# First weight slab in one load, one small row through the GpSimd queue, and a column transpose two matmuls later

## The chip, the cores and the metric

The kernel runs on one core of one Trainium2 chip. The metric is device microseconds (us) of one execution. Executions of one kernel mostly agree within 0.3%, which here is 0.6 us (the kernel before lay between 213.50 and 214.17 us in the first four runs, and between 213.33 and 213.96, 213.54 and 213.99, 213.58 and 214.00 in three later sets), and the whole change is worth less than that; so this case is also about how to measure and explain something as small as the noise.

## The reference, cut to what matters

```python
x = A_x                                        # (1, 2048, 640)
g = sigmoid((x * gate_w).sum(-1, keepdims=True))
a = ssm(x, ...)                                # a diagonal state-space scan, projections with B and C
b = gelu(x @ w1 + b1) @ w2 + b2                # w1 (640, 1728), w2 (1728, 640)
return g * a + (1 - g) * b
```

Only the first use of `x @ w1`, for the first 512 of 2048 rows of x, matters here.

## The kernel before

The program lists operations with their inputs, outputs and priorities; a small scheduler in the kernel's own code turns them into one fixed order for each engine. Work starts with loads. SyncE issues the big ones in this order: two of five column blocks of x, slab 0 of W1 in two halves, slabs 1 and 2, the other three blocks of x by a transposing load, then slabs 3 and 4. ScalarE issues five small rows. A slab is 128 rows of W1, 1024 columns wide (256 KB).

```python
load("xna", "sp", "l_xna", xn[0][:, :, 0:KN * 128], ..., ["xna"], 0, ...)
for h in range(2):
    fs = slice(h * FW // 2, (h + 1) * FW // 2)
    load(f"w1_0{h}", "sp", f"l_w10{h}", W1sb[:, 0, fs], B_w1[0:128, fs], [("w1", 0, h)], 0.1 + h, ...)
w1load(1, "sp", 1.3)
w1load(2, "sp", 2)
xtrans(0, range(KN, KD), 3, 1.8)
w1load(3, "sp", 4)
w1load(4, "sp", 5)
# ... cut ...
for i, (nm, (r0, src)) in enumerate(ROWS.items()):      # lre, lim, ldt: 5 x 128; b1a: 13 x 128
    src = src.rearrange("(k p) -> k p", p=128)
    load(nm, "act", "l_" + nm, rows[r0:r0 + src.shape[0], :], src, [nm], prio=-100 + i, dur=0.4)
load("b1b", "act", ..., ["b1b"], prio=-96, dur=0.4)      # the last 64 values of b1, twice, into one row
```

TensorE first runs seven warm-up matmuls on a constant, then transposes the two loaded blocks of x (VectorE copies them to `xT`), then begins the 40 matmuls of the first W1 stage. One further transpose, the "column transpose" (`cols`), turns the gathered rows into the per-partition columns that the activations and tables need. It waits for all five row loads.

```python
def f_warm():
    for n in (512,) * 6 + (256,):
        t = nc.tensor.matmul(PS[4][:, 0:n], one.broadcast_to([128, 128]), one.broadcast_to([128, n]), ...)
# ... cut ...
op("cols", "pe", 0.3, list(ROWS) + ["b1b", "ident"], [("bank", 7)], f_cols, prio=9.5)
# ... cut: the first W1 stage, slab by slab (k), eight column blocks (jf) in eight PSUM banks ...
seq = [(k, jf) for k in range(KD) for jf in range(NW)]
seq.remove((0, NW - 1))
seq.insert(seq.index((1, NW - 1)), (0, NW - 1))         # bank 7 is used by the column transpose first
for k, jf in seq:
    op(f"m1_0_{jf}_{k}", "pe", d_mm(512), XK0[k] + [("w1", k) if k else ("w1", 0, jf // (NW // 2))], [("bank", jf)],
       f_mm, prio=pe_prio())
```

So the order on TensorE is: 7 matmuls with slab 0, 2 with slab 1, the column transpose, 7 more with slabs 0 and 1, and then, as the **17th matmul**, the first that needs slab 2 and the transposed rest of x.

## Time and profile before

| | before |
|---|---|
| median of the first 3 runs | 214.07 us (213.73 to 214.17) |
| span of the profiled run (it was timed at 214.2 us) | 212.9 us |
| TensorE (PE) busy | 208.4 us, 98% |
| VectorE (DVE), ScalarE (ACT) busy | 188.9 us, 111.3 us |

Three lines of the page of the kernel before: its span, the busy time by engine, and the chain of work that ended last, by engine.

```profile
span 212.9 us, 3113 instructions
PE 208.4 (98%) x1254; PEld 119.8 (56%) x1264; DVE 188.9 (89%) x262; ACT 111.3 (52%) x201; POOL 2.5 (1%) x10
PE 95%; DMA 2%; issue 1%; ACTq 1%; POOL 0%; DVE 0%; POOLq 0%
```

The kernel is bound by TensorE, and the chain goes through a load for 2% of the span only. Where that load stands is told by the same chain in order of time. This is the chain of the kernel before from 2.22 to 10 us (its 16 earlier lines, GpSimd's and ScalarE's first instructions, are cut); columns are start in us, length in us, and what.

```profile
2.22 0.35 ACTq L326
2.56 0.03 issue
2.60 5.08 DMA rows<-in_B_b_dram
7.68 0.14 issue
7.82 0.22 PE ps L432
8.03 2.16 PE ps L621 x10
```

It is the load of the row `b1b`, ScalarE's fifth: issued from 2.60, landed at 7.68. After it come only matmuls, up to VectorE's last output at 210.79. Next, TensorE's timeline of the kernel before up to 10.5 us: start, length, engine, line, operation, shapes and count, and in brackets the idle time before it with what ended it. L401 are the warm-up matmuls, L413 the transposes of x, L621 the first W1 stage, L432 the column transpose.

```profile
0.78 2.93 PE L401 MATMUL ps<-const-bfloat16-1.0 128*128 128x512 bf16 x7 [0.78 <-PEq L962]
3.74 0.65 PE L413 MATMUL ps<-ident,xn 128*128 128x128 bf16 x8
4.64 1.04 PE L621 MATMUL ps<-xT,W1sb 128*128 128x512 bf16 x4 [0.25 <-DVE xT L419]
5.85 0.82 PE L621 MATMUL ps<-xT,W1sb 128*128 128x512 bf16 x3 [0.17 <-DMA W1sb<-in_B_w_dram]
6.92 0.61 PE L621 MATMUL ps<-xT,W1sb 128*128 128x512 bf16 x2 [0.25 <-DMA W1sb<-in_B_w_dram]
7.82 0.22 PE L432 MATMUL ps<-ident,rows 128*128 128x128 bf16 x1 [0.29 <-DMA rows<-in_B_b_dram]
7.87 2.97 PE L621 MATMUL ps<-xT,W1sb 128*128 128x512 bf16 x13
```

TensorE stops four times: for VectorE's copy, for the second half of slab 0 (landed at 5.80), for slab 1 (6.87) and for `b1b` (7.68). The idle times in brackets look small because a matmul's recorded length (0.379 us) overlaps the next one; matmuls that follow each other without a stop start 0.216 us apart, so the nine before the column transpose need 1.94 us and took 3.18. From 7.87 on there is no stop.

### The profile page before, as it was taken

What the parts mean: (1) busy time and instruction counts of PE and PEld (TensorE: products, weight loads), DVE (VectorE), ACT (ScalarE), POOL (GpSimd) and SP (SyncE); (2) the same over time, 40 slices, a digit from 0 to 9 for tenths busy, and PEclk for the clock granted to TensorE, in tenths of its full rate; (3) what the DMA queues carried; (4) which work ended last, traced back from release to release, by engine and by line L of the source; (5) the groups of instructions that cost most, each with busy time, mean ns of one, the idle gap of its engine ahead of it and who ended that gap; (6) DMA issues with size and microseconds to landing.
All of it is one profiled execution on the core that took longest, in us unless ns stands there. A gap on an engine that the chain in (4) does not pass through costs nothing.

```text
span 212.9 us, 3113 instructions
## 1 busy us (share of the span) xinstructions
PE 208.4 (98%) x1254; PEld 119.8 (56%) x1264; DVE 188.9 (89%) x262; ACT 111.3 (52%) x201; POOL 2.5 (1%) x10
## 2 busy tenths in 40 slices
PE   8899999999999999999999999999999999999996
PEld 3344444444467776444466777544446777767773
DVE  2399999999999999999999959999999998999343
ACT  2389556678915324556963233555793444723330
POOL 1000000000000010000000001000000000000000
DMA  5999999998100004100000004000000000000011
GB/s 134 298 284 200 170 208 318 265 222 183 22 0 3 31 31 126 62 0 0 0 3 0 0 34 155 31 31 3 0 0 2 3 31 31 31 3 31 31 34 62
DMA packets 31434, 16.35 MB, mean 77 GB/s; under 512 B 22972, under 2 KB 30652, under 8 KB 31420
## 3 DMA queue, kind: packets, MB, share of 16 engines
q1 hardware_dynamic: 31072, 14.83, 29.2%
q0 software_dynamic: 288, 1.31, 1.9%
q8 instruction: 10, 0.16, 0.3%
q14 instruction: 4, 0.03, 0.0%
q10 hardware_dynamic: 60, 0.01, 0.0%
HBM read 7.63 MB, written 2.62 MB: 48 GB/s over the span
## 4 chain that ended last, share of the span: by engine, by line
PE 95%; DMA 2%; issue 1%; ACTq 1%; POOL 0%; DVE 0%; POOLq 0%
PE ps L771 27%; PE ps L641 22%; PE ps L819 20%; PE ps L684 20%; PE ps L621 3%; DMA rows<-in_B_b_dram 2%; PE ps L785 1%; PE ps L662 1%; ACTq L326 1%; DVE osb L852 0%; POOL io_i L382 0%; PE ps L432 0%; POOL rows L372 0%; POOL st_i L384 0%; POOL st_i L383 0%
## 5 line engine op out<-in xcount | busy, mean ns | idle before, releaser
L771 PE MATMUL ps<-W2sb,Gl 128*128 128x320 bf16 x416 | 59.2, 299 | 0.0
L771 PEld LDWEIGHTS ps<-W2sb,Gl 128*128 128x128 bf16 x416 | 40.3, 98 | 17.1 <-issue 1.1
L641 PE MATMUL ps<-xT,W1sb 128*128 128x512 bf16 x215 | 47.5, 379 | 0.3
L819 PE MATMUL ps<-CT,H 128*128 128x320 bf16 (+2 forms) x320 | 45.4, 299 | 0.0
L724 DVE TENSOR_TENSOR_SCAN W<-atab,V 128x1280 bf16<-128x1280 f32 x16 | 44.3, 2811 | 0.3
L684 PE MATMUL ps<-xT,BT 128*128 128x512 bf16 x196 | 43.1, 379 | 0.3 <-issue 0.2
L819 PEld LDWEIGHTS ps<-CT,H 128*128 128x128 bf16 x320 | 31.3, 98 | 12.2
L799 ACT ACTIVATE E<-ps,g1col 128x320 bf16<-128x320 f32 x32 | 16.3, 526 | 39.7 <-PE ps L771 26.0
L641 PEld LDWEIGHTS ps<-xT,W1sb 128*128 128x128 bf16 x220 | 21.5, 98 | 26.0
L648 ACT ACTIVATE Gl<-ps,cols 128x512 bf16<-128x512 f32 x44 | 29.6, 688 | 10.0 <-PE ps L641 10.0
L684 PEld LDWEIGHTS ps<-xT,BT 128*128 128x128 bf16 x200 | 19.5, 98 | 23.5 <-ACT Gt L670 0.4
L693 ACT ACTIVATE U<-ps 128x512 bf16<-128x512 f32 x40 | 23.8, 597 | 15.0 <-PE ps L684 14.9
L830 ACT ACTIVATE E<-ps,gcol 128x320 bf16<-128x320 f32 x30 | 15.8, 527 | 22.6 <-PE ps L819 22.6
L482 DVE TENSOR_TENSOR osb<-xg,E 128x640 bf16<-128x640 bf16 x15 | 7.3, 487 | 9.2 <-ACT E L830 8.2
L758 ACT ACTIVATE ps<-b2b 128x320 f32<-128x320 bf16 x32 | 14.1, 442 | 1.1
L838 DVE SCALAR_TENSOR_TENSOR xg<-xn,gcol,dsk 128x640 bf16<-128x640 bf16 x16 | 13.9, 883 | 0.4
L598 DVE SCALAR_TENSOR_TENSOR scr<-xn,gwb 128x640 bf16<-128x640 bf16 x16 | 13.2, 823 | 0.4
L482 DVE TENSOR_TENSOR V<-V,W 128x1280 bf16<-128x1280 bf16 x16 | 12.5, 822 | 0.3
L482 DVE TENSOR_TENSOR H<-H,V 128x1280 bf16<-128x1280 bf16 x16 | 12.5, 822 | 0.3
L482 DVE TENSOR_TENSOR V<-mr,U 128x2560 bf16<-128x2560 bf16 x8 | 11.9, 1489 | 0.2
L482 DVE TENSOR_TENSOR H<-c,W 128x2560 bf16<-128x2560 bf16 x8 | 11.9, 1489 | 0.1
L482 DVE TENSOR_TENSOR V<-s,W 128x2560 bf16<-128x2560 bf16 x8 | 11.9, 1485 | 0.0
(79 smaller groups left out, 98.5 us busy)
## 6 DMA issues: line engine op xcount, KB each, us to landing
out_dram<-osb SPq DMA_DIRECT2D x15, 160.0 KB, 1.8
W2sb<-in_B_w_dram SPq DMA_DIRECT2D x1, 2080.0 KB, 9.4
xn<-in_A_x_dram POOLq DMA_DIRECT2D x2, 640.0 KB, 4.7
W1sb<-in_B_w_dram SPq DMA_DIRECT2D x4, 256.0 KB, 4.8
xn<-in_A_x_dram SPq DMA_DIRECT2D x1, 640.0 KB, 8.0
W1sb<-in_B_w_dram SPq DMA_DIRECT2D x1, 480.0 KB, 5.7
W1sb<-in_B_w_dram SPq DMA_DIRECT2D x1, 400.0 KB, 5.8
xn<-in_A_x_dram SPq DMA_DIRECT2D x1, 384.0 KB, 6.2
```

The source lines that it names most:

```text
L482: return inc("dve", nc.vector.tensor_tensor(out=o, in0=a, in1=b, op=o_))
L641: t = nc.tensor.matmul(PS[bank][:, :], W1sb[:, k, jf * 128:(jf + 1) * 128], xT[q][:, k, :], start=(k == 0), stop=(k == KD - 1))
L648: return inc("act", nc.scalar.activation(Gl[q % 2][:, jf, :], PS[bank][:, :], ACT.Gelu_apprx_tanh, bias=b1col[:, jf:jf + 1]))
L684: t = nc.tensor.matmul(PS[bank][:, :], BT[:, ci, kd, k * 128:(k + 1) * 128], xT[q][:, kd, :], start=(kd == 0), stop=(kd == KD - 1))
L693: return inc("act", nc.scalar.activation(dst, src, ACT.Copy, scale=1.0 if ci == 0 else -1.0))
L724: t = inc("dve", nc.vector.tensor_tensor_scan(out=g[:, ci, :], data0=a, data1=v[:, ci, :], initial=0.0, op0=ALU.mult, op1=ALU.add))
L758: return inc("act", nc.scalar.activation(PS[bank][:, 0:HALF], b2b[:, cols], ACT.Copy))
L771: t = nc.tensor.matmul(PS[bank][:, 0:HALF], Gl[q % 2][:, jf, t4 * 128:(t4 + 1) * 128], W2sb[:, jf, cols], start=False, stop=False, skip_gr ...
L799: return inc("act", nc.scalar.activation(E1[c % NE][:, cols], PS[bank][:, 0:HALF], ACT.Copy, scale=g1col[:, c:c + 1]))
L819: t = nc.tensor.matmul(PS[bank][:, 0:n], H[b % NHB][:, ci, k, s * 128:(s + 1) * 128], CT[:, ci, k, cols], start=(i == 0), stop=(i == 2 * K ...
L830: return inc("act", nc.scalar.activation(E2[c % NE][:, cols], PS[bank][:, 0:HALF], ACT.Copy, scale=gcol[:, c:c + 1]))
L838: return inc("dve", nc.vector.scalar_tensor_tensor(out=xg[c % 2][:, :], in0=xn[q % 2][:, c % 4, :], scalar=gcol[:, c:c + 1], in1=dsk[:, :] ...
```

## The change

The intent: fewer issues on SyncE, so that everything behind slab 0 is issued about 0.5 us earlier; `b1b` no longer last in ScalarE's queue; and the column transpose, which waits for the rows, later in TensorE's order.

```diff
-        for h in range(2):
-            fs = slice(h * FW // 2, (h + 1) * FW // 2)
-            load(f"w1_0{h}", "sp", f"l_w10{h}", W1sb[:, 0, fs], B_w1[0:128, fs], [("w1", 0, h)], 0.1 + h, dur=0.45, lat=2.0)
+        w1load(0, "sp", 1)
 ...
-        load("b1b", "act", "l_b1b", ..., ["b1b"], prio=-96, dur=0.4)
+        load("b1b", "pool", "l_b1b", ..., ["b1b"], prio=-50, dur=1.0)
 ...
-        op("cols", "pe", 0.3, list(ROWS) + ["b1b", "ident"], [("bank", 7)], f_cols, prio=9.5)
+        op("cols", "pe", 0.3, list(ROWS) + ["b1b", "ident"], [("bank", 7)], f_cols, prio=11.5)
 ...
-                op(f"m1_0_{jf}_{k}", "pe", d_mm(512), XK0[k] + [("w1", k) if k else ("w1", 0, jf // (NW // 2))], ...
+                op(f"m1_0_{jf}_{k}", "pe", d_mm(512), XK0[k] + [("w1", k)], ...
```

(Another line, in which later stages name slab 0 as an input, changes in the same way.) The order of instructions also changes in two places far from the start: VectorE's last scan comes after one combination of outputs instead of before it, and ScalarE does one small gate activation one eviction later.

More of the change, by code (lines that the diff above doesn't have):

```diff
@@ L377, in bass_gated_mix__ssm_conv_s5__dense_activation_gelu__prompt_kernel @@
             load(nm, "act", "l_" + nm, rows[r0:r0 + src.shape[0], :], src, [nm], prio=-100 + i, dur=0.4)
-        load("b1b", "act", "l_b1b", rows[RT:RT + 1, :].rearrange("o (a p) -> o a p", a=2),
-             B_b1[nmain:F].rearrange("(o p) -> o p", o=1).unsqueeze(1).broadcast_to([1, 2, FL]), ["b1b"], prio=-96, dur=0.4)
+        load("b1b", "pool", "l_b1b", rows[RT:RT + 1, :].rearrange("o (a p) -> o a p", a=2),
+             B_b1[nmain:F].rearrange("(o p) -> o p", o=1).unsqueeze(1).broadcast_to([1, 2, FL]), ["b1b"], prio=-50, dur=1.0)
         def f_iota():
@@ L622, in f_mm @@
                                                       start=(k == 0), stop=(k == KD - 1)))
-                op(f"m1_0_{jf}_{k}", "pe", d_mm(512), XK0[k] + [("w1", k) if k else ("w1", 0, jf // (NW // 2))], [("bank", jf)] ,
+                op(f"m1_0_{jf}_{k}", "pe", d_mm(512), XK0[k] + [("w1", k)], [("bank", jf)] ,
                    f_mm, prio=pe_prio())
@@ L643, in f_mm @@
                     return inc("pe", t)
-                op(f"m1_{q}_{jf}", "pe", KD * d_mm(512), XT[q] + ([("w1", 0, 0), ("w1", 0, 1)] + [("w1", k) for k in range(1, KD)] if jf < NW else [("w1", "r", int(jf * 128 >= FM))]), [("bank", bank)], f_mm, prio=pe_prio())
+                op(f"m1_{q}_{jf}", "pe", KD * d_mm(512), XT[q] + ([("w1", k) for k in range(KD)] if jf < NW else [("w1", "r", int(jf * 128 >= FM))]), [("bank", bank)], f_mm, prio=pe_prio())
                 def f_ge(jf=jf, bank=bank):
```

## The prediction

> **What bounds the kernel now.** TensorE. The page gives it 208.4 of 212.9 us busy, and the chain of waits is 95% TensorE: from 8.03 us to 210.77 us it is one unbroken run of matmuls with gaps of at most 0.16 us. The change removes no matmul, so only the first 8 us count. In the timeline, W1 matmuls start at 4.64 (released by VectorE's copy), then stop until 5.85 (second half of slab 0), until 6.92 (slab 1) and until 7.82 (the column transpose, which waits for the row b1b: the chain shows 5.08 us of DMA, from 2.60 to 7.68). Nine matmuls at 0.216 us spacing need 1.94 us and took 3.18, so 1.24 us is lost between 4.64 and 7.82.
>
> **What changes.**
> - One issue of about 0.5 us leaves SyncE's queue (each W1 issue took 0.42 to 0.49 us), so slabs 1, 2 and the x transpose are issued about 0.5 us earlier. [...] slab 1, issued at 2.26, landed at 6.87, bound by traffic more than by issue.
> - The first four matmuls lose their early release: half a landed at 4.02, the whole slab will land later. Half b landed at 5.80; I estimate the whole at 5.3 (4.8 to 5.8).
> - b1b leaves ScalarE's queue (0.68 us of issue; its table load, 3.31 to 4.59, starts that much earlier, and has slack) and goes to GpSimd after its index patterns, at about 1.4 us. GpSimd's two x loads took 0.75 to 0.89 us to issue and 1.5 us to their first packet; so first packets near 3, landing near 5 (4 to 6.5) in this traffic. [...]
> - The column transpose comes after 11 matmuls, not 9.
>
> **How much is critical.** The 17th matmul (slab 2) also needs the transposed rest of x, landed at 9.04; it began at 9.38. So gain beyond 0.34 us needs that transpose earlier, too. With slab 0 at 5.3: 16 matmuls (3.46) and the column transpose (0.05) lead to 8.85; the transpose of x, issued 0.5 earlier but in the same traffic, at 8.6 to 9.1. I expect the 17th matmul near 9.0 instead of 9.38: 0.35 us gained. The order of the last scan on VectorE also moves by about 2 us, but its H is ready 8 us before it is used: no effect.
>
> **Predicted: 213.7 us**, range 213.2 to 214.3. Faster by over 2%: 0.01; within 2%: 0.98; slower: 0.01.
>
> **What would show it.** Right: first W1 matmul about 5.3 (later than 4.64), few and shorter stops after it, no wait of the column transpose for b1b, chain of waits starting in a W1 or x load instead of b1b, everything after the 17th matmul shifted by one constant. Wrong: b1b still the last to land; slab 0 landing at or after 5.8; x transpose still at 9.0 with TensorE idle before it.
>
> **What would make it wrong.** The GpSimd load may be slow at its first use (later than 7.6 costs time one for one); the single slab may land no earlier than half b, eating the gain; the earlier table load may collide with the loads.

Slab 0 at 5.3, 16 matmuls (3.46 us) and the column transpose (0.05) come to 8.81 (8.85 stands there); with the transposed x at 8.6 to 9.1 that makes a 17th matmul near 9.0 instead of 9.38, and 0.35 us off the 214.07 us of before is 213.7. The 8.6 to 9.1 "in the same traffic" is the author's estimate; the figure of the trace that stands behind it is slab 1's in `before`: of its 4.61 us from issue to landing, issuing took 0.49.

## The result, and the profile after

| | before | after |
|---|---|---|
| median (4 runs each, taken together) | 213.9 us (213.5 to 214.17) | 213.63 us (213.47 to 213.86) |
| ratio, 95% interval | | 0.999 (0.997 to 1.001) |
| span of the profiled run | 212.9 us | 212.3 us |
| slab 0 landed (before: two halves) | 4.02 and 5.80 us | 4.33 us |
| slab 1, slab 2 landed | 6.87, 7.56 us | 6.40, 7.11 us |
| `b1b` landed | 7.68 us | 4.68 us |
| transposed x landed | 9.05 us | 8.58 us |
| 17th matmul started | 9.38 us | 8.74 us |

A ratio is the mean time of one kernel's fast runs over that of the other's of the same rounds, so it is not quite the ratio of the medians quoted. Times here are rounded; the recorded texts cut some of them (9.047 us stands there as 9.04, 8.186 us as 8.18).

The page of the changed kernel, the same three lines:

```profile
span 212.3 us, 3122 instructions
PE 209.3 (99%) x1264; PEld 120.6 (57%) x1264; DVE 189.2 (89%) x262; ACT 111.3 (52%) x201; POOL 3.0 (1%) x11
PE 99%; DVE 0%; issue 0%
```

(This trace holds 1264 PE records and that of before 1254, with 1264 weight loads in both: ten matmul records of before are missing, so the busy times are not compared.) The chain of the changed kernel in order of time, first 10 us:

```profile
0.78 2.93 PE ps L399 x7
3.71 0.03 issue
3.75 1.03 PE ps L411 x8
4.78 2.99 PE ps L619 x11
7.77 0.06 PE ps L430
7.83 2.37 PE ps L619 x11
```

And TensorE's timeline of the changed kernel, first 10.5 us (L399 is the warm-up, L411 the transposes of x, L619 the W1 stage, L430 the column transpose):

```profile
0.78 2.93 PE L399 MATMUL ps<-const-bfloat16-1.0 128*128 128x512 bf16 x7 [0.78 <-PEq L960]
3.75 1.03 PE L411 MATMUL ps<-ident,xn 128*128 128x128 bf16 x8
4.74 3.03 PE L619 MATMUL ps<-xT,W1sb 128*128 128x512 bf16 x11
7.61 0.22 PE L430 MATMUL ps<-ident,rows 128*128 128x128 bf16 x1
7.67 3.18 PE L619 MATMUL ps<-xT,W1sb 128*128 128x512 bf16 x14
```

All waits for loads are gone: the chain is TensorE alone from 0.78 us, and neither `b1b` nor a slab is in it. The transposing load of x was issued 0.49 us earlier, as SyncE's lines of the two kernels show, the kernel before first:

```profile
3.27 1.54 SPq L333 DMA_TRANSPOSE xT<-in_A_x_dram  x1
2.78 1.49 SPq L333 DMA_TRANSPOSE xT<-in_A_x_dram  x1
```

TensorE's lines hide a second thing. The eight transposes of x took 1.03 us where they took 0.65 before, and eleven matmuls took 3.03 us from 4.74, where eleven at 0.216 us spacing plus the overlap of the last (0.379 minus 0.216) would take 2.54. The starts of single instructions show why: the transposes started 107 ns apart (56 before), and the first W1 matmuls at 4.74, 5.14, 5.57, 5.88 and then every 0.216 us. TensorE ran at half speed until about 5.8 us in this run, and until about 3.8 us in the run of before, with the same warm-up from 0.78 us. The granted clock that the profile lists is 1.00 for both kernels and in every stretch of the first 10 us, but it says nothing here: the traces of these two runs hold no clock record at all, and the profile lists 1.00 all the same, also from 4 to 6 us in the changed kernel, where matmuls started 0.40 and 0.43 us apart. Nine of the 14 traces do hold clock records (not `before`, `after`, `after_again`, `slab_only` and `after_cold`); the first one lies between 3.97 and 9.38 us, in each of the nine where the spacing of the matmuls changes (in `before_again`, for instance, at 5.13). So the spacing is a true reading of the speed.

### The profile page after: what moved, and what is told of

Read it like the earlier page. It is cut to its first block, busy times and chain, and to the rows that moved or that the text cites. A ratio compares the mean times of both kernels' runs of the same rounds, so it can differ in the third digit from the quotient of the medians.

```text
span 212.3 us, 3122 instructions
## 1 busy us (share of the span) xinstructions
PE 209.3 (99%) x1264; PEld 120.6 (57%) x1264; DVE 189.2 (89%) x262; ACT 111.3 (52%) x201; POOL 3.0 (1%) x11
## 3 DMA queue, kind: packets, MB, share of 16 engines
HBM read 7.63 MB, written 2.62 MB: 48 GB/s over the span
## 4 chain that ended last, share of the span: by engine, by line
PE 99%; DVE 0%; issue 0%
PE ps L769 27%; PE ps L639 22%; PE ps L817 20%; PE ps L682 20%; PE ps L619 4%; PE ps L399 1%; PE ps L783 1%; PE ps L660 1%; PE ps L411 0%; DVE osb L850 0%; PE ps L430 0%
## 5 line engine op out<-in xcount | busy, mean ns | idle before, releaser
L639 PE MATMUL ps<-xT,W1sb 128*128 128x512 bf16 x220 | 48.1, 379 | 0.0
L682 PE MATMUL ps<-xT,BT 128*128 128x512 bf16 x200 | 43.8, 379 | 0.0
```

The lines of the kernel that those rows point to most:

```text
L639: t = nc.tensor.matmul(PS[bank][:, :], W1sb[:, k, jf * 128:(jf + 1) * 128], xT[q][:, k, :], start=(k == 0), stop=(k == KD - 1))
L682: t = nc.tensor.matmul(PS[bank][:, :], BT[:, ci, kd, k * 128:(k + 1) * 128], xT[q][:, kd, :], start=(kd == 0), stop=(kd == KD - 1))
```

## The experiments

Three theories were set against each other.

- **A (gates).** The 17th matmul starts when the last of its gates opens: TensorE's own earlier matmuls, slab 1 or 2, the row loads through the column transpose, or the transposed x. The whole time is that start plus a constant.
- **B (clock).** The moment when TensorE reaches full speed differs from run to run and eats the gain.
- **C (noise).** The 0.6 us between the two profiled spans is chance.

Later ones (D, E, F, P, S) are stated with their runs. A ratio's partner is the 9 to 11 runs of the kernel before. Kernels are compared only within the same rounds.

### 1. The changed kernel again: `after_again`

No edit. Expected:

> The changed kernel unaltered, for a firmer ratio and a second look at its start. Its profile had the transposes of x and the first three W1 matmuls at half speed (107 and about 420 ns apart instead of 56 and 216), until about 5.8 us; in the kernel before the full speed came at about 3.8 us. Theory A (gates): the 17th matmul waits for the transposed rest of x (landed 8.58) and the speed matters little; gain 0.5 to 0.7 us every time. Theory B [...] where it is late the 17th matmul starts at 9.0 or later and the gain is gone; then the runs of this kernel spread by 0.5 us or more. Rival C (noise): ratio within 0.999 to 1.001 and no lasting difference of the 17th matmul's start.

Measured: median 213.48 us (213.16 to 213.81), ratio 0.9986 (0.9973 to 0.9998). TensorE's timeline of this run, the first eleven W1 matmuls:

```profile
4.60 1.68 PE L619 MATMUL ps<-xT,W1sb 128*128 128x512 bf16 x7 [0.25 <-DVE xT L417]
6.54 1.04 PE L619 MATMUL ps<-xT,W1sb 128*128 128x512 bf16 x4 [0.26 <-DMA W1sb<-in_B_w_dram]
```

Here TensorE was at full speed from the first transposes (55 ns apart), ran out of work and waited for slab 1 (landed at 6.49), and the 17th matmul started at 8.70, 0.05 us after the transposed x landed (8.65). In the first run of this kernel it was slow until 5.8, waited for nothing, and started the 17th at 8.74, 0.16 us after the transposed x (8.58). So a full speed that comes 2 us later cost at most about 0.1 us: it used up time that would have been spent waiting. B's moment does differ from run to run, but it does not eat the gain. The interval just leaves out 1, so C is weakened but the effect is small.

The wait for the transposed x has no bracket in the timeline and is missing from the chain of waits, which runs on from slab 1's load: a matmul's recorded length of 0.379 us covers any stop of up to 0.16 us. It shows in the start of the 17th matmul, 0.367 us after the 16th, and in the waits of TensorE's weight loads (who waited, for what, us in total, times, longest):

```profile
PEld ps L619 <- DMA xT<-in_A_x_dram: 0.5, 1, 0.5
```

### 2. Each part alone: `slab_only`, `b1b_only`, `cols_only`

`slab_only` takes the first and last hunk of the diff, `b1b_only` the second, `cols_only` the third, each on the kernel before. Expected, in this order:

> Slab 0 in one load, the rest as before. Theory A: slab 0 lands near 4.3 to 4.5, the transposed x about 0.5 us earlier (near 8.6), but the column transpose still stands after 9 matmuls and waits for b1b, which still lands at 7 to 7.7; the 17th matmul starts 1.7 us after that, at 8.8 to 9.4; gain 0 to 0.4 us, most likely 0.1. If b1b lands well before 7 here, its wait was caused by the split slab. C: no change at all.

> b1b through GpSimd, the rest as before. Theory A: b1b lands near 4.7, the column transpose no longer waits; the two halves of slab 0 still land at 4.0 and 5.8, slab 1 at 6.9, so TensorE still stops twice; the 17th matmul is then held by the transposed x at 9.0: gain 0.2 to 0.35 us. C: no change.

> Only the column transpose two matmuls later. Theory A: TensorE does two more matmuls (0.43 us) in the time in which it waited for b1b (landing 7.7), so the column transpose starts at 7.8 as before and five matmuls are left instead of seven; the 17th matmul is then held by the transposed x at 9.0 to 9.1: gain 0.3 us, as much as either other part alone. C: no change.

Measured, with landings from the one profiled run of each:

| kernel | median us | ratio (95% interval) | b1b landed | column transpose | transposed x landed | 17th matmul |
|---|---|---|---|---|---|---|
| `slab_only` | 213.64 | 0.9996 (0.9984 to 1.0009) | 6.78 | 7.08 | 8.19 | 8.65 |
| `b1b_only` | 213.93 | 1.0000 (0.9987 to 1.0014) | 4.28 | 7.38 | 9.08 | 9.13 |
| `cols_only` | 213.61 | 0.9993 (0.9981 to 1.0006) | 7.59 | 7.73 | 8.95 | 9.00 |

`b1b` landed at 6.78 in `slab_only`, earlier than the expected 7 to 7.7. In the profiled runs the gates are where A put them: with `b1b` early, or with two more matmuls ahead of the column transpose, the 17th matmul starts 0.05 us after the transposed x; with the slab alone, it starts after the column transpose and seven matmuls (7.08 + 0.06 + 7 x 0.216 = 8.65). But the slab alone did not meet the gate that A had named for it. The column transpose did not wait for `b1b`: it started 0.216 us after the matmul before it, and its line has no bracket:

```profile
7.08 0.22 PE L430 MATMUL ps<-ident,rows 128*128 128x128 bf16 x1
```

The last gate there was TensorE itself, which ran without a stop but at half speed until about 5.7 us. The timed gains of the parts are not resolved: all three intervals hold 1 and also hold a gain of 0.25 us. The 0.2 to 0.35 expected of `b1b_only` and the 0.3 expected of `cols_only` were not seen in the means.

### 3. Two parts at a time: `slab_cols`, `slab_b1b`

`slab_cols` is the whole change without the `b1b` hunk, `slab_b1b` the whole change without the column hunk. Expected:

> The change without its GpSimd part: slab 0 in one load, column transpose after 11 matmuls, b1b on ScalarE's queue. With slab 0 in one load b1b landed at 6.78 even on ScalarE's queue (7.68 with the split slab), before eleven matmuls are done (7.0 to 7.6). Theory A (the 17th matmul starts when the last of its gates opens, the time is that start plus 203.5 us): the 17th matmul starts at 8.2 to 8.7, as early as in the whole change or up to 0.4 us earlier; time equal to the whole change or 0.1 to 0.4 us less. Rival D (the GpSimd part is needed for the gain): b1b lands at 7.6 again, 17th matmul at 9.0, no better than the column shift alone.

> The change without its column shift: slab 0 in one load and b1b through GpSimd, column transpose after 9 matmuls. Theory A: the rows that stay on ScalarE's queue land at 5.8 to 6.0, nine matmuls are done at 6.6 to 7.1, so nothing waits and the 17th matmul starts with the transposed x at 8.6 to 8.7, as in the whole change: the shift is worth nothing once b1b comes early. Also: slab 1, slab 2 and the transposed x landed 0.4 to 0.5 us later in both looks at the whole change (8.58, 8.65) than in the single-slab kernel (8.18); if the GpSimd load causes that, 8.6 again here; if it was chance, something near 8.2 is as likely.

Measured: `slab_cols` median 213.36 us, ratio 0.9986 (0.9974 to 0.9997); `slab_b1b` 213.33 us, 0.9984 (0.9972 to 0.9996). In their profiled runs the 17th matmul started at 8.64 (transposed x 8.60) and 8.42 (transposed x 8.36; a tie, for TensorE's own matmuls allowed no start before 8.42 either). D falls: with the slab in one load, either of the other two parts gives what both give, as far as these intervals tell, and the GpSimd route is not needed. That the slab alone gives less is not shown: its interval overlaps theirs. The question whether the GpSimd load itself delays the big loads stays open: 8.36 is between the two values that were named.

### 4. The kernel before again: `before_again`

No edit. Expected:

> The kernel before, unaltered, as one of the four: it tells how far two equal kernels differ here, and gives a second look at its start. Its nine runs in the last call spanned 212.0 to 212.6 us, the 17th matmul at 9.38 in the one look belongs to a run of 212.9. Theory A: time minus the 17th matmul's start is 203.5 us here too, so a faster run must show b1b or the transposed x landing earlier (b1b 7.0, 17th matmul 8.7 to 9.0). Ratio within 0.999 to 1.001.

Measured: median 213.75 us, ratio 1.0001 (0.9989 to 1.0013): two equal kernels. One line of TensorE's timeline in this run, the column transpose:

```profile
7.32 0.22 PE L432 MATMUL ps<-ident,rows 128*128 128x128 bf16 x1 [0.29 <-DMA rows<-in_B_b_dram]
```

The wait for `b1b` is there again, with the same 0.29 us in brackets, but everything is 0.5 us earlier than in the first profile: `b1b` at 7.18 (7.68), transposed x at 8.55 (9.05), 17th matmul at 8.88 (9.38), span 212.4 (212.9). This unaltered kernel thus differs from itself by 0.5 us at the start. In both runs the 17th matmul started about 0.33 us after the transposed x, held by `b1b`.

### 5. Another order of the loads: `after_xt_first`

```diff
-        xtrans(0, range(KN, KD), 3, 1.8)
+        xtrans(0, range(KN, KD), 1.9, 1.8)      # on the changed kernel: before slab 2, not after it
```

> The changed kernel with the transposed load of x issued before slab 2 instead of after it. Theory A: the transposed x lands about 0.7 us earlier (near 7.9) and slab 2 then lands last, near 8.4 to 8.7, so the gate moves to slab 2 and the 17th matmul starts at 8.4 to 8.8: no or little gain. If the loads land by issue order at one common rate, the later of the two lands at the same 8.6. A 17th matmul at 8.2 or earlier would say that the transposed load itself, not the sum of the traffic, was the limit.

Measured: median 213.95 us, ratio 1.0006 (0.9993 to 1.0019), with one run at 214.74. The transposed x landed at 7.76, as expected, but slab 2 at 9.80 in the profiled run, so the 17th matmul came at 9.93. TensorE's timeline there:

```profile
7.56 1.24 PE L619 MATMUL ps<-xT,W1sb 128*128 128x512 bf16 x5
9.93 1.24 PE L619 MATMUL ps<-xT,W1sb 128*128 128x512 bf16 x5 [1.13 <-DMA W1sb<-in_B_w_dram]
```

The expected 8.4 to 8.8 was missed by 1.1 us: the loads do not simply share one rate. The transposed load kept SyncE's queue busy from 2.26 to 4.42 us (such a first transposing load took from 1.49 us (`after`) to 2.88 us (`b1b_first`) to issue in ten runs, slabs 0 to 2 and their halves 0.42 to 0.49 us each in `before` and `after`), so slab 2 was issued at 4.47 instead of 2.27, and it landed 5.3 us after that (4.8 us after its issue in the changed kernel). By their spans the other four runs were better (212.3 to 212.9). This is no improvement.

### 6. What stops the W1 loads: `rows_pool`

In the changed kernel all rows go through GpSimd, so ScalarE issues no load early:

```diff
-            load(nm, "act", "l_" + nm, ..., [nm], prio=-100 + i, dur=0.4)
+            load(nm, "pool", "l_" + nm, ..., [nm], prio=-49 + i, dur=0.1)
```

> The changed kernel with all five row loads on GpSimd's queue, so that ScalarE issues no load in the first 8 us. In every look so far the big loads nearly stop between 3.6 and 4.6 us (packets of 2 KB fall from about 40 to 8 to 20 in 0.2 us and some take 0.3 to 1.4 us), while ScalarE's row packets of 256 bytes come through. Theory E (the row loads of ScalarE hold the W1 loads up, and this is the part of the slab that I mis-sized): no such stop, slab 1 lands at 5.0 to 5.5 instead of 5.8 to 6.5, the transposed x at 7.4 to 8.0, the 17th matmul at 8.1 to 8.3 unless the rows, now issued until about 4.5, land after 7.4. Rival F (the stop belongs to the W1 loads themselves or to the memory): the stop stays, slab 1 at 5.8 to 6.5, transposed x at 8.2 to 8.6, 17th matmul at 8.4 to 8.7. It also bears on the hope that this version beats both: E says 0.3 us less than the whole change.

Measured: median 214.63 us, ratio 1.0045 (1.0032 to 1.0058). TensorE's timeline:

```profile
4.88 2.60 PE L619 MATMUL ps<-xT,W1sb 128*128 128x512 bf16 x11
8.58 0.22 PE L430 MATMUL ps<-ident,rows 128*128 128x128 bf16 x1 [1.10 <-DMA rows<-in_B_b_dram]
```

E falls. Slab 1 landed at 6.04 and the transposed x at 8.50, within what F said; between 3.8 and 4.8 us the trace has 13 to 27 of the 2 KB packets in each 0.2 us (7 to 17 in the changed kernel, against 38 to 41 just before the stop in that kernel), so the stop is milder at most; in `slab_b1b`, where ScalarE does issue its rows, it was as mild (13 to 31). GpSimd issues its loads one after the other, 0.5 to 0.7 us each; the last, issued at 3.69, landed at 8.29, and the column transpose waited for it: 1 us lost. The hope for a better version was wrong.

### 7. Is it the place in the queue: `b1b_first`

In the kernel before, `b1b` becomes the first of ScalarE's five loads:

```diff
-             ..., ["b1b"], prio=-96, dur=0.4)
+             ..., ["b1b"], prio=-101, dur=0.4)
```

> The kernel before with b1b as the first of ScalarE's five loads instead of the last; nothing else. Theory P (b1b was late because it was the last of the queue): the load that is now last, the long row b1, lands at 7.0 to 7.7, and the column transpose waits as before: same time as before. Rival S (b1b was late for its own form[...]): b1b lands late or lands near 3, and the long row lands at 5.2 to 5.6 as before, so the column transpose no longer waits: 17th matmul held by the transposed x, gain about 0.2 us as the GpSimd route alone was to have.

Measured: median 213.84 us, ratio 1.0007 (0.9993 to 1.0020). `b1b` landed at 3.60, and the long row `b1a`, now the last, at 6.99 (5.21 before). The column transpose waited for it and started at 7.24. P holds: whichever of the two stood last in that queue was late, and `b1b` has no fault of its own form. Whether it is the last place or the later issue (3.21 instead of 2.22 us), just before the big loads slow down, was not separated.

### 8. The clock: `after_cold`, `before_cold`

Six of the seven warm-up matmuls are taken out of the changed kernel and of the kernel before (only the 256-column one is left):

```diff
-            for n in (512,) * 6 + (256,):
+            for n in (256,):
```

> The changed kernel without six of the seven warm-up matmuls, to see what the speed of TensorE's clock is worth at the start. Theory B [...]: the transposes of x and the first 8 to 14 W1 matmuls run at half speed (107 and 427 ns apart), full speed comes at 7 to 10 us, the 17th matmul starts at 9.3 to 11; 0.7 to 2 us slower than the changed kernel. If the warm-up does nothing: same time.

> The same for the kernel before. Theory B: slower than before by 0.3 to 1.7 us, a little less than the changed kernel loses, because its waits for loads hide part of the slow matmuls; the two cold kernels then differ by less than 0.3 us.

Measured: `after_cold` 214.65 us, ratio 1.0037 (1.0019 to 1.0055); `before_cold` 214.63 us, 1.0048 (1.0033 to 1.0063). TensorE's timeline of `before_cold`:

```profile
3.68 1.03 PE L413 MATMUL ps<-ident,xn 128*128 128x128 bf16 x8 [2.53 <-DMA xn<-in_A_x_dram]
4.67 4.02 PE L621 MATMUL ps<-xT,W1sb 128*128 128x512 bf16 x9
8.49 0.31 PE L432 MATMUL ps<-ident,rows 128*128 128x128 bf16 x1
```

Nine W1 matmuls without a stop take 4.02 us, 427 ns from start to start. The full speed came at about 7.7 us in `after_cold` and 9.4 us in `before_cold` (the expected 7 to 10 was the author's estimate), and TensorE's own slow work became the gate (transposed x at 8.08 and 8.36, 17th matmul at 9.68 and 10.50). Against the warm kernel of the same kind the warm-up is worth about 1 us. Without it the two medians are equal, but the means, 214.54 and 214.77 us, differ by as much as those of the warm kernels, and with four runs each the intervals overlap. Whether the change still wins without the warm-up is open.

The spacings are of two kinds: transposes of x started 107 ns (`after`) or 56 ns (`before`) apart, W1 matmuls 427 ns (`before_cold`) or 216 ns apart. What sets the moment of the full speed was not shown. With the same warm-up from 0.78 us it had come by 3.8 us in `before` and `after_again` and only at 5.8 us in `after`, that is up to 3.0 and 5.0 us into the work.

### All profiled runs together

The strongest support for A: the one profiled run behind each of the 14 labels (12 kernels, two of them twice).

| run | row that landed last | transposed x | column transpose | 17th matmul | span | span minus 17th |
|---|---|---|---|---|---|---|
| before | 7.68 | 9.05 | 7.82 | 9.38 | 212.88 | 203.50 |
| before_again | 7.18 | 8.55 | 7.32 | 8.88 | 212.38 | 203.50 |
| b1b_only | 5.43 | 9.08 | 7.38 | 9.13 | 212.64 | 203.51 |
| cols_only | 7.59 | 8.95 | 7.73 | 9.00 | 212.51 | 203.51 |
| b1b_first | 6.99 | 8.26 | 7.24 | 8.80 | 212.29 | 203.49 |
| before_cold | 7.01 | 8.36 | 8.49 | 10.50 | 214.00 | 203.50 |
| after | 6.02 | 8.58 | 7.61 | 8.74 | 212.25 | 203.51 |
| after_again | 5.80 | 8.65 | 7.42 | 8.70 | 212.21 | 203.51 |
| slab_only | 6.78 | 8.19 | 7.08 | 8.65 | 212.15 | 203.50 |
| slab_cols | 7.18 | 8.60 | 7.34 | 8.64 | 212.16 | 203.52 |
| slab_b1b | 5.17 | 8.36 | 6.85 | 8.42 | 211.93 | 203.51 |
| after_xt_first | 6.12 | 7.76 | 7.50 | 9.93 | 213.43 | 203.50 |
| rows_pool | 8.29 | 8.50 | 8.58 | 9.71 | 213.22 | 203.51 |
| after_cold | 5.16 | 8.08 | 8.55 | 9.68 | 213.20 | 203.52 |

The last column is constant to 0.02 us while the start moves by 2 us. The start itself follows the gates: in 12 of the 14 runs it is, to 0.01 us, the later of two times, the landing of the transposed x plus 0.047 us, and the start of the column transpose plus 0.056 us plus 0.216 us for each matmul that still comes before the 17th (seven, or five where the transpose was moved). The other two are `before_cold`, where some of these matmuls ran at half speed, and `after_xt_first`, where slab 2 came last. Each timed run also has a span, to 0.1 us, so each can be read as a start of the 17th matmul (its span minus 203.5): the 34 later runs of the kernel before lie between 8.5 and 9.2, mean 8.89; the nine of the changed kernel between 8.3 and 9.0, mean 8.70. Two things follow. The gain is about 0.2 us. And the profile of before from which the prediction was read, with 9.38, was a slower start than any of those 34 runs.

## Why the prediction was right or wrong

The predicted time, 213.7 us (213.2 to 214.3, within 2%), holds: 213.63 measured, and 213.48 in the second set. This is no strong test, because the range also holds the kernel before (213.9): the number would have been called right without any gain. The steps tell more.

- **What bounds it, and that only the first 8 us count: right.** The constant 203.5 us shows it. The moved scan on VectorE had no effect, as predicted: it started at 187.05 instead of 185.04, its H was done at 197.1, and the chain of the changed kernel reaches the projection that may use it at 204.69.
- **The column transpose waited for `b1b`, and the 17th matmul is limited by the transposed x: right, unless TensorE is slow.** In four runs (`b1b_only`, `cols_only`, `after_again`, `slab_cols`) the 17th matmul started 0.05 us after the transposed x landed and more than 0.35 us after the 16th, so it waited for that load; in `slab_b1b` the two gates tied. In `after` and `slab_only` TensorE, at half speed until 5.8 and 5.7 us, was itself the last gate, 0.16 and 0.47 us after the transposed x.
- **The size of the gain: roughly right, for partly the wrong reason.** The step "I expect the 17th matmul near 9.0 instead of 9.38: 0.35 us gained" gave 8.74 in the profile, 0.64 us, more than predicted; by the means of the timed runs it is 8.70 instead of 8.89, and 0.22 and 0.25 us of time in the two sets (means 213.87 to 213.65 and 213.73 to 213.48). The starting point, 9.38, came from one profile, and that run happened to be late. The prediction thus overstated the gain of the means and understated that of the two profiles; that its time still came within 0.1 us of the measured one is in part luck.
- **Slab 0's landing, "I estimate the whole at 5.3 (4.8 to 5.8)": wrong in size.** It landed at 4.33 in both runs, only 0.3 us after the half did (4.02), so the first W1 matmul was not delayed to 5.3; it started at 4.74, held by VectorE's copy as before. The estimate rested on half b landing at 5.80. But in the experiments the stop near 3.6 to 4.6 us hit whatever came second: half b with the split slab (5.4 to 5.8), slab 1 with the whole one (5.8 to 6.5). What causes the stop was not found; ScalarE's row loads alone are ruled out by `rows_pool`.
- **The GpSimd load, "landing near 5": right.** 4.68 and 4.51. In `after` its first data packet came at 3.74, 2.28 us after the start of its issue, and the increments of its semaphore lie between 4.24 and 4.68; those of the ScalarE load in `before` lie at 3.71, 7.63 and 7.68. As the first of its queue this load landed 2.6 us after the start of its issue on ScalarE (`b1b_first`) and 2.8 to 3.2 us after it on GpSimd (`b1b_only`, `after_again`, `after`).
- **"Chain of waits starting in a W1 or x load": half right.** In `after` there was no load in the chain at all, because TensorE was slow; in `after_again`, at full speed, the listed chain starts in slab 1's load, and the last wait, for the transposed x, is the one that it leaves out.
- **The earlier issue, "slabs 1, 2 and the x transpose are issued about 0.5 us earlier": right, and it was worth more than I allowed.** The transposed x was issued at 2.78 instead of 3.27; it landed at 8.08 to 8.65 in seven runs with the whole slab (mean 8.42, without the reordered kernel) and at 8.36 to 9.08 in five with the split one (mean 8.80, without `b1b_first`). The ranges overlap, so the 0.4 us is likely rather than shown.
- **TensorE's speed at the start was missing from the prediction.** It changed what the profile looked like more than it changed the time.

The reason why no single part gave a resolved gain fits A, but is argued rather than shown: the whole slab moves the transposed x, and the other two parts remove the wait for `b1b`, which in the kernel before opened 0.33 us after it; a part that moves only one of two gates gains at most their difference. It does not explain everything. If the 0.33 us were typical, removing the wait alone should gain about 0.29 us, as much as the whole change; yet `b1b_only` was 0.09 us slower in the mean and `cols_only` 0.10 us faster. The spans, read as starts, suggest gates closer together: 8.86 for the kernel before in that call, 8.88, 8.94 and 8.82 for `slab_only`, `b1b_only` and `cols_only`, 8.64 for the whole change. How the gates stand in runs that were not profiled is open.

## What to carry to other kernels

Where a kernel is one unbroken run of matmuls after its start, find the first matmul of that run, list what must be there for it, and note that the gate which opens last is all that counts; then the span minus that start is a constant (here 203.49 to 203.52 us in 14 profiles), and each timed run becomes a measurement of the start. Read such starts from several profiles before you predict a change of tenths of a microsecond: here one unaltered kernel differed from itself by 0.5 us. A load that is small is not early: the last of ScalarE's five landed 4.2 to 5.1 us after its issue (3.8 when another row took the last place; 4.6 for the last of five on GpSimd, in `rows_pool`), and with the slab in one load, moving its consumer back two matmuls could not be told from moving the load (ratios 0.9986 and 0.9984).
